# Attention and a gated MLP in one kernel: the first batch taken in one piece, two of its head groups paired

## The chip, the cores and the metric

The kernel runs on one core of one Trainium2 chip. The metric is device time in microseconds (us), the median over runs of the whole kernel. Before the change it is 391.98 us (three runs, 391.68 to 392.12).

## The reference

```python
scores = (1/sqrt(64)) * q @ k.T            # 8 batches, 12 heads, 448 tokens, 64 wide
attn   = exp(scores) / sum(exp(scores))    # the maximum is subtracted first
x      = (attn @ v) as (8*448, 768)        # tokens by all heads
h      = x @ w_in                          # 768 -> 2048
out    = (h * sigmoid(h)) @ w_out          # 2048 -> 768
```

Inputs and output are float32. The kernel loads them as float16 and gathers sums in float32.

## The kernel before

**Work.** Batches are taken one after the other. The 12 heads of a batch form three head groups of four heads (`HG = 4`, `NG = 3`). K and Q of a group are loaded with heads and 32 rows on the partitions, and VectorE turns them (`turn_k` L315, `turn_q` L333). The 448 keys form four chunks (`NCH = 4`).

**Attention of one unit.** A unit is a batch, a head group and a stretch of queries. For each key chunk, TensorE computes scores (`score`, L346) into one of two score tiles, each for two heads; ScalarE takes the exponential of each tile (`expo`, L383) into a tile `E`. A burst of scores can be *whole* (both score tiles, four heads side by side in four row strips of the array) or a *half* (one tile, two heads side by side). A half streams as many columns through the array as a whole one and does half of the work; units below `HALVES` go in halves. Then come three passes with four heads side by side in four column strips (`attend`, L409): sums (weights are ones) and two value passes (`part` 1 and 2, weights are V). VectorE turns the sums, takes the reciprocal, turns it back (L450, L458, L464) and multiplies it into the value passes (`norm`, L480), which gives the tile `xT`.

**Lone and paired head groups.** A *lone* group (`LONES`, numbered `3 * batch + group`) has its own four chunks: eight half or four whole bursts, and three passes of four chunks. In a *pair*, each group has three chunks of its own, and the fourth chunk is shared: 64 keys of each (`scores_rest`). VectorE adds the three E tiles of a group (`add_e`, L394), so the sums of both groups take three matmul steps (`attend_sums`, L425). Before the change groups 0 to 3 are lone: batch 0 and the first group of batch 1.

**Batch 0.** Its queries are cut into two pieces of 224 (`PIECES`), so it has six units of 224 queries, all lone. A burst covers two chunks (`per_burst`). Units 0 to 5 go in halves.

**The MLP.** `ffn1` multiplies `xT` by w_in in 16 blocks `f` of six matmuls each (L492, by way of `times`); ScalarE takes tanh (L518), VectorE multiplies (`gate`, L553). Batch 0 does this once for each piece, 224 columns at a time. The second product (`plain`, then `product`, also L492) goes to the output. With `strips` set, a matmul over 128 weight columns is cut into four of 32 columns, which run side by side; this avoids a change of the array's mode next to the passes of attention.

**What sets the order.** The order of all instructions is fixed when the kernel is built: `Order` keeps assumed durations and due times for TensorE, ScalarE, VectorE and the loads, and the loop at the end always issues what its clock says is ready. Each engine then runs its list strictly in that order and waits where data is late. While TensorE would have nothing to do before the first `ffn1`, the loop issues matmuls of zeros (`run_zeros`, L1468). All loads go through POOL's queue in the order of the `plan_k`, `plan_q`, `plan_v`, `plan_w_in`, `plan_w_out` calls; the queue has eight counters, so a load waits until the load eight places ahead of it has landed. V of batch 0 comes as four loads for all three groups.

```python
if qk is not None and qk <= od.now and (od.now >= pace["next"] or moe_i is None):
    run_qk()                          # a burst of scores
elif moe_i is None and av is not None and av <= od.now:
    run_av()                          # a pass of sums or values
```

Of the kernel before, what the change touches and what calls it, by code (L numbers as in the profile page):

```python
# [17 lines left out]
PE_OUT = 0.20  # L18
HOP = 0.10
DMA_ROW = 0.022  # L20
DMA_RATE = 13570.0
# [60 lines left out]
class Order:  # L82
# [19 lines left out]
    def start(self, op):  # L102
        self.emit(op.emit)
        self.free[op.eng] = self.now + op.busy
        self.busy[op.eng] += op.busy
        op.done = self.now + op.busy + op.tail
        if op.then:
            op.then(op.done)
# [61 lines left out]
def kernel(  # L170
# [29 lines left out]
    PACE = 2.6  # L200
    LONES = (0, 1, 2, 3)
    NPL = 4
    EAGER = 1
    HALVES = 6
    NEAR, LATE = 0.15, -2.0
# [4 lines left out]
    TWB, SXB = 40, 4  # L210
    PIECES = ((0, 7), (7, TPP))
    NE, NX3, NT_ = 9, 6, 2
# [129 lines left out]
    def score(pS, n, c, e, h, x0, x1, p0):  # L342
        b, hg, g0, g1 = units[n]
        nq = 32 * (g1 - g0)
        at = nq * (c % per_burst(n))
        nc.tensor.matmul(  # L346
            out=pS[p0 : p0 + 32 * (x1 - x0), h % 2, at : at + nq],
            lhsT=KT[(b, hg)][32 * h : 32 * (h + 1), c, x0:x1, :, e],
            rhs=QT[n][32 * h : 32 * (h + 1), e],
            start=(e == 0),  # L350
            stop=(e == 1),
        )


    def per_burst(n):
        return 2 if units[n][0] == 0 else 1

    def scores(n, w, ys):
        score_banks(n, w, ys)
        for c in range(per_burst(n) * w, per_burst(n) * (w + 1)):  # L360
            for e in range(2):
                for y in ys:
                    for h in (2 * y, 2 * y + 1):
                        score(pS_t[(n, w, y)], n, c, e, h, 0, rows_of(n, c) // 32, 0)


    def scores_rest(n):
        score_banks(n, 3, (0, 1))
        for e in range(2):
            for h in range(HG):  # L370
                pS = pS_t[(n, 3, h // 2)]
                score(pS, n, 3, e, h, 0, 2, 0)
                score(pS, n + 1, 3, e, h, 2, 4, 64)
# [4 lines left out]
    def expo(n, w, y):  # L378
        kr = rows_of(n, w * per_burst(n))
        nk = 32 * (units[n][3] - units[n][2]) * per_burst(n)  # L380
        if (n, w) not in E:
            E[(n, w)] = sb.tile([128, HG, S], FP16, name=f"E_{n}_{w}", tag="E", bufs=NE)
        nc.scalar.activation(  # L383
            out=E[(n, w)][0:kr, 2 * y : 2 * y + 2, 0:nk],
            in_=pS_t[(n, w, y)][0:kr, :, 0:nk],
            func=AF.Exp,
            scale=attn_scale,
        )
# [12 lines left out]
    def attend_mm(a, n, part, c, h, k0, k1, e, start, stop):  # L401
        b, hg, g0, g1 = units[n]
        nq = 32 * (g1 - g0)
        at = nq * (c % per_burst(n))
        if part == 0:
            w = ones[k0:k1, :]
        else:
            w = VT[b][k0:k1, HG * hg + h, c, part - 1 :: 2]
        nc.tensor.matmul(  # L409
            out=a[32 * h : 32 * (h + 1), 0:nq],  # L410
            lhsT=w,
            rhs=e[k0:k1, h, at : at + nq],
            start=start,
            stop=stop,
        )
# [16 lines left out]

    def attend(ns, part, n):
        if part == 0 and len(ns) == 2:
            attend_sums(ns)
            return
        acc[(n, part)] = ps.tile([128, 512], FP32, name=f"a_{n}_{part}", tag="m", bufs=4)
        for c in range(NCH):
            e = E[(ns[0] if c == NCH - 1 else n, c // per_burst(n))]
            for h in range(HG):  # L440
                attend_mm(
                    acc[(n, part)], n, part, c, h, 0, rows_of(n, c), e, c == 0, c == NCH - 1
                )
# [335 lines left out]
    for b in range(B):  # L779
        for g0, g1 in PIECES if b == 0 else ((0, TPP),):  # L780
            units += [(b, hg, g0, g1) for hg in range(NG)]
    NU = len(units)
# [38 lines left out]

    NB0 = NG * len(PIECES)
    for hg in range(NG):
        plan_k(0, hg)
        plan_q(hg)
    plan_v(0, 0, NG)
    plan_q(NG)
    plan_q(NG + 1)
    plan_w_in(0, DFF // 2)
    plan_q(NG + 2)  # L830
    plan_k(1, 0)
    plan_q(NB0)
    plan_w_in(DFF // 2, DFF)
    plan_k(1, 1)
    plan_q(NB0 + 1)
    plan_w_out(0, NFF // 4)
    plan_w_out(NFF // 4, NFF // 2)
    plan_k(1, 2)
    plan_q(NB0 + 2)
    for hg in range(NG):  # L840
        plan_v(1, hg, hg + 1)
    plan_w_out(NFF // 2, 3 * NFF // 4)
    plan_w_out(3 * NFF // 4, NFF)
    for n in range(NB0 + NG, NU):
        b, hg = units[n][:2]
        plan_k(b, hg)
        plan_q(n)
        plan_v(b, hg, hg + 1)
# [222 lines left out]
    def sums_w(ms):  # L1071

        for m in ms:
            w_op[m] = [
                od.add(
                    Op(
                        "DVE",
                        0.9,
                        lambda m=m, f0=f0: combine_w(m, f0, f0 + 4),
                        ld_wout  # L1080
                        + list(plain_op.values()) * (m == 7)
                        + [w_op[k][f0 // 4] for k in {6: (5,), 4: (6,)}.get(m, ())],
                        30,
                    )
                )
                for f0 in (0, 4)
            ]

    def queue_plain(t, j):
# [6 lines left out]
        def queue(f0, f1):  # L1096
# [17 lines left out]
            def deps():  # L1114
                if len(parts) < f0 // NPL:
                    return [None]
                made = [ld_wout[i] for i in range(len(ld_wout)) if wout_rows[i] < f1]
                for f in range(f0, f1):
                    x = g_op.get((0, f), ())
                    if len(x) < len(PIECES):  # L1120
                        return [None]
                    made += x
                return made
# [19 lines left out]
    def plan_sums():  # L1143
# [4 lines left out]
        if len(todo) == 4:  # L1148
            gates = {}
            for b in batches(qd):  # L1150
                for f in range(NFF):
                    if len(g_op.get((b, f), ())) < (len(PIECES) if b == 0 else 1):
                        return
                    gates.setdefault(f, []).extend(g_op[(b, f)])
            gates_of[qd] = gates
        gates = gates_of[qd]
        while todo and (todo[0] == 7 or sg_ring.can(1, od.now)):
# [4 lines left out]
            for f0 in (0, 4):  # L1162
                deps = [x for f in range(f0, f0 + 4) for x in gates[f] + gates[f + HF]]
                if m != 5:
# [4 lines left out]
                            "DVE",  # L1169
                            0.34,  # L1170
                            lambda m=m, f0=f0: combine_g(qd, m, f0, f0 + 4),
# [116 lines left out]
    for ns in jobs:  # L1288
        if len(ns) == 1:
            split = ((0,), (1,)) if ns[0] < HALVES else ((0, 1),)  # L1290
            qk_seq += [(ns, c, ys) for c in range(NCH // per_burst(ns[0])) for ys in split]
        else:
            split = ((0,), (1,)) if ns[0] < HALVES else ((0, 1),)
            qk_seq += [([n], c, ys) for n in ns for c in range(NCH - 1) for ys in split]
            qk_seq.append((ns, 3, (0, 1)))
        av_seq += [(ns, 0, ns[0])] + [(ns, part, n) for n in ns for part in (1, 2)]
    pace = {"next": 0.0}
# [18 lines left out]
    def run_qk():  # L1316
# [4 lines left out]
        if ys[0] == 0:  # L1321
# [3 lines left out]
            "PE",  # L1325
            2 * per_burst(n) * mm(nq) + (0.03 if rest else 0.013),
            (lambda: scores_rest(n)) if rest else (lambda: scores(n, c, ys)),
            tail=PE_OUT,
        )
        op.half = len(ys) == 1  # L1330
        if c == NCH // per_burst(n) - 1 and ys[-1] == 1:
            done = []
# [6 lines left out]
        for y in ys:  # L1339
            made = od.add(  # L1340
                Op(
                    "ACT",
                    act(2 * nq * per_burst(n)),
                    lambda y=y: expo(n, c, y),
                    [op],
                    tail=0.2,
                    then=s_ring.give,
# [25 lines left out]
    def av_at():  # L1373
        if not av_seq:
            return None
        ns, part, n = av_seq[0]
        if len(ns) == 2 and part == 0:
# [6 lines left out]
        deps = []  # L1384
        if len(exp_op.get(n, ())) < 2 * NCH // per_burst(n):
            return None
        for i, x in enumerate(exp_op[n]):
            deps.append((x, i // 2 * per_burst(n) * mm(32 * (units[n][3] - units[n][2]))))
        if part:
            deps += [(x, LATE * (units[n][0] == 0)) for x in ld_v[units[n][:2]]]  # L1390
            if units[n][0] > 0:
                deps += [(x, 0.9) for x in rdn_op.get(n, [None])]
        at, m = when(deps), m_ring.when(1)
        return None if at is None or m is None else max(at, m)

    def run_av():
        ns, part, n = av_seq.pop(0)
        b, hg, g0, g1 = units[n]
        nq = 32 * (g1 - g0)
        two = len(ns) == 2  # L1400
        m_ring.take()
        op = Op(
            "PE",
            (3 if two and part == 0 else 4) * mm(nq) + 0.013,
            lambda: attend(ns, part, n),
            tail=PE_OUT,
        )
        if part == 2:

            def then(at):  # L1410
                for _ in range((3 + (n == ns[1])) if two else NCH // per_burst(n)):
                    e_ring.give(at)
# [7 lines left out]
        if part == 0:  # L1420
            after_sums(ns, op, nq)
        else:
            after_av(n, part, op, nq)
# [135 lines left out]
```

## Time and profile before

| what | us |
|---|---|
| median of the runs shown | 391.98 |
| the profiled execution | 392.65 |
| its span (first to last instruction) | 390.8 |
| TensorE (PE) busy | 384.9 |
| VectorE (DVE) busy | 274.6 |
| ScalarE (ACT) busy | 253.8 |
| matmuls of zeros, on the chain that ended last | 2% of the span |

The profiled execution took 1.85 us more than its span, and 0.67 us more than the median. PE means matmuls, PEld weight loads, POOL the engine that issues the loads. In a row of the timeline the first number is the start, the second the time until the last of the group has ended; a group's last matmul ends some 0.2 us after the next group may start, because matmuls are pipelined. The granted TensorE clock is 1.00 in every stage.

### The profile page before, as it was taken

What the parts mean: (1) busy time and instruction counts of PE and PEld (TensorE: products, weight loads), DVE (VectorE), ACT (ScalarE), POOL (GpSimd) and SP (SyncE); (2) the same over time, 40 slices, a digit from 0 to 9 for tenths busy, and PEclk for the clock granted to TensorE, in tenths of its full rate; (3) what the DMA queues carried; (4) which work ended last, traced back from release to release, by engine and by line L of the source; (5) the groups of instructions that cost most, each with busy time, mean ns of one, the idle gap of its engine ahead of it and who ended that gap; (6) DMA issues with size and microseconds to landing.
All of it is one profiled execution on the core that took longest, in us unless ns stands there. A gap on an engine that the chain in (4) does not pass through costs nothing.

```text
span 390.8 us, 10670 instructions
## 1 busy us (share of the span) xinstructions
PE 384.9 (98%) x4369; PEld 206.8 (53%) x4369; DVE 274.6 (70%) x570; ACT 253.8 (65%) x399; POOL 89.1 (23%) x173
## 2 busy tenths in 40 slices
PE   8999999999999999999999999999999999999995
PEld 7657774444444444545445444544445655556663
DVE  2466676999996887887678758666869984447441
ACT  4987885697875779666674766566793338892120
POOL 6632456415006242400643015000000000000000
PEclk9999999999999999999999999999999999999999
DMA  7999999929039582914856129102100131001333
GB/s 116 202 210 210 162 166 180 182 43 142 3 56 148 118 109 37 129 41 93 129 92 89 47 68 164 16 0 54 32 0 3 39 92 33 0 1 38 91 96 102
DMA packets 35330, 34.52 MB, mean 88 GB/s; under 512 B 11345, under 2 KB 33745, under 8 KB 35281
## 3 DMA queue, kind: packets, MB, share of 16 engines
q0 software_dynamic: 24784, 22.82, 39.7%
q1 hardware_dynamic: 10080, 10.53, 9.9%
q8 instruction: 34, 0.56, 0.6%
q10 hardware_dynamic: 416, 0.49, 0.4%
q14 instruction: 16, 0.12, 0.1%
HBM read 45.61 MB, written 11.01 MB: 145 GB/s over the span
## 4 chain that ended last, share of the span: by engine, by line
PE 98%; ACT 1%; issue 0%; DVE 0%
PE p L492 31%; PE h L492 29%; PE s L346 13%; PE a L409 11%; PE f L492 8%; PE o L492 3%; PE z L1468 2%; PE a L425 2%; ACT E L383 1%; ACT ost L768 0%; ACT th L518 0%; DVE zeros L228 0%
## 5 line engine op out<-in xcount | busy, mean ns | idle before, releaser
L383 ACT ACTIVATE E<-s 128x896 f16<-128x896 f32 (+1 forms) x172 | 149.8, 915 | 38.5 <-PE s L346 37.0
L492 PE MATMUL h<-xT,w_in_t 128*32 128x448 f16 (+2 forms) x1086 | 117.1, 336 | 0.0
L492 PEld LDWEIGHTS <-w_in_t 128*128 128x128 f16 (+1 forms) x1158 | 71.1, 97 | 56.3 <-issue 11.5
L518 ACT ACTIVATE th<-h 128x448 f16<-128x448 f32 (+1 forms) x112 | 54.2, 493 | 36.7 <-PE h L492 31.0
L553 DVE SCALAR_TENSOR_TENSOR G<-th,h 128x448 f16<-128x448 f16 (+2 forms) x112 | 55.6, 508 | 23.4 <-ACT th L518 21.7
L492 PEld LDWEIGHTS <-G 128*128 128x128 f16 (+1 forms) x580 | 43.1, 98 | 32.4 <-issue 4.6
L768 ACT COPY ost<-p 128x384 f32<-128x384 f32 x52 | 25.0, 480 | 53.5 <-PE p L492 47.1
L346 PE MATMUL s<-rq,KT 32*128 32x448 f16 (+4 forms) x768 | 51.0, 338 | 0.5 <-ACT E L383 0.4
L280 POOL DMA_DIRECT2D V<-in_v_dram x88 | 48.3, 559 | 13.6 <-DMA w_out_t<-in_moe_w_out_dram 6.5
L492 PE MATMUL p<-w_out_t,G 128*128 128x384 f16 (+1 forms) x352 | 49.5, 326 | 0.0
L409 PE MATMUL a<-E,V 128*32 128x448 f16 (+2 forms) x864 | 42.3, 333 | 0.0
L492 PEld LDWEIGHTS <-S 128*128 128x128 f16 (+1 forms) x408 | 30.0, 98 | 22.7 <-issue 2.3
L261 POOL DMA_DIRECT2D rq<-in_q_dram x27 | 15.1, 558 | 103.9 <-PE s L346 83.1
L492 PE MATMUL p<-D,S 128*128 128x384 f16 (+1 forms) x256 | 37.1, 326 | 0.0
L480 DVE SCALAR_TENSOR_TENSOR xT<-a,rdn 128x448 f16<-128x448 f32 (+1 forms) x54 | 30.4, 568 | 6.4 <-PE a L409 4.4
L774 DVE TENSOR_TENSOR ost<-p,ost 128x384 f32<-128x384 f32 x39 | 21.6, 554 | 18.7 <-PE p L492 13.6
L346 PEld LDWEIGHTS <-KT 32*128 32x128 f16 (+2 forms) x864 | 17.5, 99 | 28.9 <-issue 27.6
L409 PEld LDWEIGHTS <-V 128*32 128x32 f16 (+1 forms) x864 | 20.5, 96 | 18.8 <-issue 7.6
L394 DVE TENSOR_TENSOR T<-E,E 128x1792 f16<-128x1792 f16 x20 | 21.7, 1083 | 8.1 <-ACT E L383 7.9
L394 DVE TENSOR_TENSOR T<-T,E 128x1792 f16<-128x1792 f16 x20 | 21.7, 1083 | 5.7 <-ACT E L383 5.7
L315 DVE STREAM_TRANSPOSE KT<-rk 128x256 f32<-128x256 f32 (+3 forms) x48 | 16.6, 384 | 7.2 <-DMA rk<-in_k_dram 6.4
L492 PE MATMUL p<-w_out_t,S 128*128 128x384 f16 (+1 forms) x152 | 19.1, 326 | 0.0
(67 smaller groups left out, 321.9 us busy)
## 6 DMA issues: line engine op xcount, KB each, us to landing
out_dram<-ost SPq DMA_DIRECT2D x194, 48.0 KB, 1.6
rk<-in_k_dram POOLq DMA_DIRECT2D x24, 224.0 KB, 5.6
rq<-in_q_dram POOLq DMA_DIRECT2D x21, 224.0 KB, 5.8
w_in_t<-in_moe_w_in_dram POOLq DMA_DIRECT2D x6, 512.0 KB, 11.1
w_out_t<-in_moe_w_out_dram POOLq DMA_DIRECT2D x4, 768.0 KB, 13.5
V<-in_v_dram POOLq DMA_DIRECT2D x43, 64.0 KB, 3.9
V<-in_v_dram POOLq DMA_DIRECT2D x40, 48.0 KB, 4.2
rq<-in_q_dram POOLq DMA_DIRECT2D x6, 112.0 KB, 6.1
```

The source lines that it names most:

```text
L280: nc.gpsimd.dma_start(out=VT[b][32 * x : 32 * (x + 1), hs, 0:count, :], in_=v[b, hs].rearrange("h (i g) d -> i h g d", g=TPP)[:, :, first ...
L315: nc.vector.transpose(out=pairs[:, x:y, 0:count], in_=t[:, first : first + count * (y - x)].rearrange("p (x c) i -> p x c i", c=count),)
L346: nc.tensor.matmul(out=pS[p0 : p0 + 32 * (x1 - x0), h % 2, at : at + nq], lhsT=KT[(b, hg)][32 * h : 32 * (h + 1), c, x0:x1, :, e], rhs=QT[ ...
L383: nc.scalar.activation(out=E[(n, w)][0:kr, 2 * y : 2 * y + 2, 0:nk], in_=pS_t[(n, w, y)][0:kr, :, 0:nk], func=AF.Exp, scale=attn_scale,)
L394: nc.vector.tensor_tensor(out=T[n], in0=T[n] if step else E[(n, 0)], in1=E[(n, step + 1)], op=ALU.add,)
L409: nc.tensor.matmul(out=a[32 * h : 32 * (h + 1), 0:nq], lhsT=w, rhs=e[k0:k1, h, at : at + nq], start=start, stop=stop,)
L480: nc.vector.scalar_tensor_tensor(out=x3(b, cc)[:, cc % 3, 32 * g0 : 32 * g1], in0=acc[(n, part)][:, 0:nq], scalar=0.5, in1=rdn_t[n].rearra ...
L492: nc.tensor.matmul(out=out[i : i + cut], lhsT=w[:, i : i + cut], rhs=x, start=start, stop=stop, skip_group_check=True,)
L518: nc.scalar.activation(out=th, in_=h_t[(b, f, t0)][:, 0 : t1 - t0], func=AF.Tanh)
L553: nc.vector.scalar_tensor_tensor(out=dst[:, f, at + lo : at + hi], in0=th_t[(b, f, t0)][:, lo - t0 : hi - t0], scalar=1.0, in1=h_t[(b, f, ...
L768: nc.scalar.copy(out=ost(qd, *OUT[m]), in_=bank(qd, BANK[m]))
L774: nc.vector.tensor_tensor(out=t, in0=bank(qd, BANK[m]), in1=t, op=ALU.add)
```

## The change

- `PIECES` and `per_burst` go. Batch 0 has three units of 448 queries, a burst covers one chunk, and each block of `ffn1` for batch 0 is 448 columns wide.
- `LONES` becomes (2, 3): groups 0 and 1 of batch 0 are a pair, group 2 is lone. `HALVES` becomes 3 (the three units of batch 0), and the shared chunk of the first pair goes in halves too.
- V of batch 0 is loaded by head group. Loads come in the order K0 Q0 K1 Q1 V0 V1 K2 Q2, half of w_in, V2, then K and Q of batch 1, the rest of w_in, and on as before.
- `attend` takes a range of chunks. The value passes of the first pair's first unit are cut: chunks 0 to 2 of both are listed ahead of the pair's sums, the shared chunk after them.
- The assumed durations of the order change: work on ACT and DVE may start 0.09 and 0.07 us before its predecessor ends (`OVERLAP`), an exponential's result counts 0.06 us after its end and no longer 0.2, and `combine_w` and `combine_g` take 0.95 and 0.40 and no longer 0.9 and 0.34.

```diff
+OVERLAP = {"ACT": 0.09, "DVE": 0.07}
...
-        self.free[op.eng] = self.now + op.busy
+        self.free[op.eng] = self.now + op.busy - OVERLAP.get(op.eng, 0.0)
...
-    LONES = (0, 1, 2, 3)
+    LONES = (2, 3)
...
-    HALVES = 6
+    HALVES = 3
...
-    PIECES = ((0, 7), (7, TPP))
...
-    def scores_rest(n):
-        score_banks(n, 3, (0, 1))
+    def scores_rest(n, ys):
+        score_banks(n, 3, ys)
         for e in range(2):
-            for h in range(HG):
+            for h in range(2 * ys[0], 2 * ys[-1] + 2):
...
-    def attend(ns, part, n):
+    def attend(ns, part, n, c0, c1):
...
-    for hg in range(NG):
+    for hg in range(2):
         plan_k(0, hg)
         plan_q(hg)
-    plan_v(0, 0, NG)
+    for hg in range(2):
+        plan_v(0, hg, hg + 1)
+    plan_k(0, 2)
+    plan_q(2)
+    plan_w_in(0, DFF // 2)
+    plan_v(0, 2, 3)
+    plan_k(1, 0)
     plan_q(NG)
-    plan_q(NG + 1)
-    plan_w_in(0, DFF // 2)
-    plan_q(NG + 2)
-    plan_k(1, 0)
-    plan_q(NB0)
     plan_w_in(DFF // 2, DFF)
...
-            qk_seq.append((ns, 3, (0, 1)))
-        av_seq += [(ns, 0, ns[0])] + [(ns, part, n) for n in ns for part in (1, 2)]
+            qk_seq += [(ns, 3, ys) for ys in split]
+        whole = [(ns, part, n, 0, NCH) for n in ns for part in (1, 2)]
+        if ns[0] == 0:
+            av_seq += [(ns, part, 0, 0, NCH - 1) for part in (1, 2)]
+            whole[:2] = [(ns, part, 0, NCH - 1, NCH) for part in (1, 2)]
+        av_seq += [(ns, 0, ns[0], 0, NCH)] + whole
...
-                    tail=0.2,
+                    tail=0.06,
```

## The prediction

> **What bounds the kernel now.** First I read the engines' busy times and the chain that ended last: TensorE is 98% of both. Next the waits of TensorE over the whole span, which are three, and none after 28.7 us. So beyond the first stage the time is what TensorE has to stream, and only the first stage is open to something else. Its timeline is next.
>
> ```profile
> PE 98%; ACT 1%; issue 0%; DVE 0%
> ```
> ```profile
> PE z L1468 <- DVE zeros L228: 1.0, 1, 1.0
> PE a L409 <- issue: 0.5, 1, 0.5
> PE s L346 <- ACT E L383: 0.4, 1, 0.4
> ```
> ```profile
> 13.27 0.57 PE L346 MATMUL s<-rq,KT 32*128 32x224 f16 x8
> 13.77 0.40 PE L1468 MATMUL z<-zeros 128*128 128x128 f16 x4
> 14.10 0.57 PE L346 MATMUL s<-rq,KT 32*128 32x224 f16 x8
> ...
> 16.27 0.57 PE L409 MATMUL a<-E,V 128*32 128x224 f16 x16
> 16.77 0.57 PE L346 MATMUL s<-rq,KT 32*128 32x224 f16 x8
> ...
> 30.31 0.75 PE L492 MATMUL h<-xT,w_in_t 128*128 128x224 f16 x6
> ```
>
> The reader is to see three prices. A half burst (8 matmuls of 224, two side by side) streams 896 columns, 0.373 us at 2400 columns per us, and the next group starts 0.50 us after it: a change of the array's mode costs some 0.12. A pass of 16 also takes 0.50. Four zeros and a change take 0.33. And the first MLP matmul (h) stands at 30.31: the border between the two stages. The chain of waits gives the dense prices:
>
> ```profile
> 203.11 3.40 PE h L492 x72
> ...
> 206.51 3.03 PE a L409 x64
> ...
> 318.75 31.21 PE f L492 x165
> ...
> 351.83 35.11 PE p L492 x216
> ```
>
> 72 column-strip matmuls of 448 are 18 steps of 0.189 us: 0.1867 of columns and 0.0026 more. The last matmul ends at 351.83 + 35.11 = 386.94.
>
> **Part one: from the first h to the end.** I count the instruction lists of both kernels, columns divided by how many matmuls run side by side. Before: 332.05 us of columns, 1994 steps, 158 changes of mode. With 0.0026 a step (5.2 us) the measured 386.94 - 30.31 = 356.63 leaves 19.4 us, 0.123 a change; the 13.77 row agrees. After: 330.56 us, 1884 steps, 155 changes. The difference is -1.49 - 0.29 - 0.37 = **-2.15 us**. It has plain sources. Before, the last piece's three passes (12 steps of 224, 1.12 us) still lie behind the first h, and so does the first burst of batch 1 (0.37); after, both lie ahead of it. The 110 steps are these 14 and the 96 that vanish as `ffn1` of batch 0 goes 448 wide. All later batches have the same columns; only their order differs.
>
> What must keep up there: ACT has 16 tanh of 0.546 in place of 32 of 0.363, 2.9 us less. Two exponentials take 1.73 and can start 0.67 after their burst (25.08 to 25.75), so a burst needs 2.4 from the one before. Batch 1's bursts stand at least 2.6 apart (two h blocks of 1.14 and a burst, or one and a pass). DVE's gates are 16 of 0.615 in place of 32 of 0.382. I cost both at nothing; TensorE's own work is the cover, 0.2 us at its thinnest. If that cover fails on all six bursts of batch 1's first pair, it is about 1 us.
>
> **Part two: up to the first h.** TensorE's list ahead of it streams 14.37 us in place of 14.56. Pairing takes one chunk in eight off, 22 half bursts for 24, and one step in four off the pair's sums. Against that come the passes and the burst of batch 1 named above, the zeros 51 + 48 for 47 + 40, and 43 changes of mode for 49. After: 1.0 (the start) + 51 x 0.109 (the first zeros, 5.13 us for 47) + 48 x 0.053 + 14.37 + 0.2 + 43 x 0.123 = 29.0 us if nothing waits. The same sum before is 29.25, and the measured 30.31 has 1.06 of waits. So I walk after's list with ACT beside it: exponentials 0.83 apart (five in 4.17, the last 0.915), the first 0.67 after its burst. ACT's timeline has that pace:
>
> ```profile
> 6.86 4.17 ACT L383 ACTIVATE E<-s 128x896 f16<-128x896 f32 x5 [4.83 <-PE s L346]
> ```
>
> - Q0 comes whole, 224 KB for 112. K0 had landed by 4.85; by bytes (368 KB moved by 5 us, 150 a us then) Q0 lands near 6.6. Its turn is 0.63 (row: 0.619), so the first burst stands at 7.3, not 6.13, and the zeros end at 6.6: 0.6 of waiting.
> - The first six exponentials pace TensorE: 7.95 to 13.0, 0.6 of waiting in spite of the zeros.
> - The seventh burst follows at 12.25, and then the first early value pass (three steps, 0.57) at 13.0, held by the sixth exponential and by V0, next paragraph.
> - From there TensorE is the slower of the two: a burst and a pass are 1.2 us, and ACT's 22nd exponential starts at 27.1, not at the 25.5 that 0.83 apart would give. Waits sum to 0.5.
> - The pair's sums need both T tiles (four adds of 1.083, two behind the sixth exponential, two behind the twelfth, ready at 19.9) and are reached at 20.1. The turn, reciprocal and turns back (0.65, 0.32, two of 0.62) hide behind the 18th burst; the lone group's chain and its last norm (0.62) end at 31.2, and the sixth matmul of h needs that at 31.6.
>
> h then starts at 29.0 + 1.7 = 30.7 us: **+0.4**. The early drawing of the two passes is in this: it fills 0.55 each where zeros would stand.
>
> **The loads.** POOL's order ahead of w_in now is K0 Q0 K1 Q1, four V0, four V1, K2, Q2, and each waits for the load eight ahead. In POOL's timeline of before, the eleventh load (a Q) shows such a wait, for the second K, the third load:
>
> ```profile
> 8.54 0.57 POOL L261 DMA_DIRECT2D rq<-in_q_dram  x1 [1.47 <-DMA rk<-in_k_dram]
> ```
>
> V0's last byte is the 1147th KB; before moved that much by 9.9, and its four first V loads landed some 1.6 us after their byte (issue to landing 7.4 and 7.9). So V0 is there at 11.5, for 13.0. K2 is issued at 11.2, when its counter is free; the first K took 3.6 from issue to landing, so 14.8, Q2 0.8 later; by the walk they delay nothing up to 16.5 and 17.3. The queue may run dry from 10.4 to 12.2, and then all later loads land about 1 us later. K and Q of batch 1 (24.9, 26.1 before) are wanted at 28.5. w_in's halves (23.7, 33.6) at 30.7 and 43. w_out's second half (issued 49.0 and 49.8, 7.5 and 10.9 to landing: 57.3, 61.5) at 59.7 and 64.3. All are covered, w_out by 1.4 us when the shift is taken off. The extra memsets (two of 0.31) and five more POOL issues (eight V more, three Q fewer, 0.55 each) lie in POOL's own time: it waits on counters there.
>
> **Sum.** -2.15 + 0.4 = -1.75: a span of 389.05 and, with the 1.85 outside it, 390.9 for the profiled execution, which was 392.65. The median shown stands 0.67 below that: 391.98 - 1.75 = **390.2**. The walk's own bounds: no waiting at all gives h at 29.0 and 388.5; each 1 us of later V0, K2 or w_out adds up to 1 us.
>
> [...] 72 more steps of h and 20 of o go in column strips, 8 of p fewer. By the rows a strip step costs 0.189, as the whole one does (165 f in 31.21 us), so this costs nothing. [...] Were four strip loads of 97 ns (row: L492 PEld 128*32, mean 97) to stand one behind the other, a step would need 0.39 us; 84 more such steps would add 17 us, 407. The 203.11 row says they do not: 72 strips in 3.40.
>
> **The rivals.**
> - *V0 or K2 late* (slower). Place: the seventh burst is followed, on TensorE's strict list, by the pass that waits for all four V0 loads; all bursts and so all exponentials queue behind it. Beyond 13.0 us each us costs one. For: small V loads had up to 11.1 to landing (one of 32 KB), and V0's last is issued near 5.5, so 16.6 and +3.6: 393.8. Likewise K2 by the 8.6 median of K loads in the first 45 us: 19.8, +3.1, 393.3. It turns the sign when V0 is later than 14.8 or K2 than 18.3. Against: in this stretch loads follow their bytes. 0.13.
> - *The first stage does not wait.* Q0 lands with K0 and the walk's 0.6 + 0.6 shrink: 388.5 to 389.5. Against: ACT's pace of 0.83 and 22 exponentials. 0.16.
> - *The gain is given back later.* A list made with other durations lets TensorE wait for ACT, DVE or w_out somewhere in 300 us, where before it waits nowhere: 1 to 2 us, 391.2 to 392.2. For: exponentials now count 0.14 sooner. Against: TensorE's changes cost 0.123 where the order assumes 0.094, so over 155 of them the other engines gain room. 0.15.
> - *The strips' weights*: 407. 0.01.
> - *Forecast*, 389.5 to 391.1: 0.55.
>
> **Chances and range.** 0.2% is 0.8 us, about what a measurement of this kernel can tell from no change. Faster by more: the forecast, the early start, and a little of the give-back: 0.72. Within: most of the give-back, 0.14. Slower: 0.14. The range holds the forecast, the early start's upper half and the give-back: 388.9 to 392.2.
>
> **What would show it.** Right: h starts near 30.7; the first burst near 7.3; the first value pass near 13.0 without a wait for V; from h to the last matmul 354.5 us with no TensorE wait; the ACT row of exponentials back to back only up to the seventh. Wrong: a TensorE wait for a V or K load before 20 us, a wait at o near 59 or 64 us, or waits for ACT between h blocks.

## The result and the profile after

The changed kernel takes 393.85 us (median of 19 executions, 391.93 to 398.41); the kernel before, beside it, takes 392.07 (19 executions, 391.65 to 392.49). The ratio is 1.0057, with a 95% interval of 1.0041 to 1.0074: slower by 0.6%, where 390.2 was forecast. The spread is the first oddity: 6.5 us, where before has 0.8. This ratio and the later ones leave out executions more than 1.5% above the fastest of their kernel, here the two at 398.37 and 398.41.

The profiled execution took 395.92, its span 394.1. Its chain that ended last, and its waits of TensorE, look nearly as before; only 2% of the span now belong to a DMA, 4.15 us of it to the landing of the very first Q:

```profile
PE 95%; DMA 2%; DVE 1%; ACT 1%; issue 1%; POOL 0%; DVEq 0%; POOLq 0%
```
```profile
PE s L344 <- DVE rq L333: 1.1, 1, 1.1
PE z L1468 <- DVE zeros L228: 1.0, 1, 1.0
PE s L344 <- ACT E L377: 0.6, 1, 0.6
```

By this view TensorE waits no longer than 0.2 us anywhere behind 9 us (the fourth row, for VectorE, in the dense part). The chain in order of time runs through TensorE alone from 8.39 us to the first MLP matmul, but for one exponential of 0.93. Still that matmul is late. The timeline of TensorE (start, duration, then line, operation, tile and count):

```profile
6.82 0.58 PE L344 MATMUL s<-rq,KT 32*128 32x448 f16 x8 [1.05 <-DVE rq L333]
...
10.82 0.57 PE L344 MATMUL s<-rq,KT 32*128 32x448 f16 x4
11.33 0.35 PE L1468 MATMUL z<-zeros 128*128 128x128 f16 x3
11.63 0.93 PE L344 MATMUL s<-rq,KT 32*128 32x448 f16 x4
12.49 0.29 PE L1468 MATMUL z<-zeros 128*128 128x128 f16 x1
12.71 1.31 PE L402 MATMUL a<-E,V 128*32 128x448 f16 x12
...
35.88 1.30 PE L488 MATMUL h<-xT,w_in_t 128*128 128x448 f16 x6
```
```profile
355.15 35.12 PE p L488 x216
```

h stands at 35.88 and not at 30.7. From there to the last matmul (355.15 + 35.12 = 390.27, by the chain) it is 354.39. The third and fifth row show the same burst, four matmuls of 448, once in 0.57 and once in 0.93 us: TensorE itself became slow. The clock row of the page (forty slices of 9.85 us) and the windows say how (columns: busy time and instructions of PE, PEld, DVE, ACT and POOL, then the granted clock, the DMA share, GB/s):

```profile
PEclk9559999999999999999999999999999999999999
```
```profile
8.00:12.00 4.00, 3.57 (x30) 1.39 (x29) 2.23 (x4) 4.00 (x6) 1.81 (x4) 0.94 0.98 128
12.00:16.00 4.00, 4.00 (x37) 0.83 (x33) 1.57 (x3) 2.39 (x4) 4.00 (x7) 0.50 0.99 143
16.00:20.00 4.00, 4.00 (x26) 1.21 (x22) 2.05 (x4) 2.64 (x4) 1.20 (x3) 0.50 0.98 139
20.00:24.00 4.00, 4.00 (x33) 1.11 (x34) 1.09 (x1) 2.82 (x4) 0.55 (x1) 0.50 1.12 208
```

The granted clock is exactly half from 12 us on; in finer windows it falls at 11.53 and returns at 28.60. In before it is 1.00 there:

```profile
8.00:12.00 4.00, 4.00 (x67) 2.55 (x64) 2.65 (x9) 3.70 (x5) 2.55 (x5) 1.00 1.33 187
12.00:16.00 4.00, 4.00 (x60) 2.75 (x62) 1.18 (x3) 4.00 (x6) 1.79 (x3) 1.00 1.31 204
16.00:20.00 4.00, 4.00 (x100) 2.53 (x96) 1.81 (x5) 3.71 (x5) 2.62 (x4) 1.00 1.12 209
```

The last column is the second thing to see: loads move 128, 143 and 139 GB/s from 8 to 20 us, where before moved 187, 204 and 209. Over the three windows that is 0.76 MB less in 12 us, some 3.6 us of loading at 209.

The mean granted clock of each execution sorts the 19: 14 lie below 0.995, five at 0.996 or more. A mean of 0.998 can still be the full clock in the first stage: a profiled execution with that mean (e10 below) shows 1.00 in every window from 4 to 36 us. The three at 0.998 or more took 391.93, 393.10 and 393.66. So a second loss is there at full clock too.

### The profile page after: what moved, and what is told of

Its sections match the earlier page's. It is cut to its first block, busy times and chain, and to the rows that moved or that the text cites. A ratio compares the mean times of both kernels' runs of the same rounds, so it can differ in the third digit from the quotient of the medians.

```text
span 394.1 us, 10432 instructions
## 1 busy us (share of the span) xinstructions
PE 387.3 (98%) x4277; PEld 191.4 (49%) x4277; DVE 272.0 (69%) x538; ACT 249.7 (63%) x381; POOL 92.0 (23%) x180
## 4 chain that ended last, share of the span: by engine, by line
PE 95%; DMA 2%; DVE 1%; ACT 1%; issue 1%; POOL 0%; DVEq 0%; POOLq 0%
PE p L488 29%; PE h L488 28%; PE s L344 13%; PE a L402 10%; PE f L488 8%; PE o L488 3%; DMA rq<-in_q_dram 2%; PE a L418 2%; PE z L1468 1%; ACT E L377 0%; DVE rq L333 0%; POOL rk L255 0%; DVE sT L446 0%; DVE ost L770 0%; ACT ost L764 0%
## 5 line engine op out<-in xcount | busy, mean ns | idle before, releaser
L377 ACT ACTIVATE E<-s 128x896 f16<-128x896 f32 (+1 forms) x170 | 146.8, 915 | 39.3 <-PE s L344 38.7
L488 PE MATMUL h<-xT,w_in_t 128*32 128x448 f16 (+1 forms) x1206 | 116.6, 353 | 0.0
L488 PEld LDWEIGHTS <-w_in_t 128*32 128x32 f16 (+1 forms) x1278 | 62.9, 97 | 62.6 <-issue 10.3
L514 ACT ACTIVATE th<-h 128x448 f16<-128x448 f32 x96 | 52.4, 545 | 36.4 <-PE h L488 32.7
L549 DVE SCALAR_TENSOR_TENSOR G<-th,h 128x448 f16<-128x448 f16 (+1 forms) x96 | 53.7, 567 | 22.3 <-ACT th L514 21.2
L280 POOL DMA_DIRECT2D V<-in_v_dram x96 | 52.3, 553 | 18.6 <-DMA w_out_t<-in_moe_w_out_dram 6.0
L344 PE MATMUL s<-rq,KT 32*128 32x448 f16 (+2 forms) x672 | 50.9, 379 | 1.8 <-DVE rq L333 1.1
L402 PE MATMUL a<-E,V 128*32 128x448 f16 (+1 forms) x768 | 43.7, 368 | 0.2 <-DVE ost L770 0.2
L476 DVE SCALAR_TENSOR_TENSOR xT<-a,rdn 128x448 f16<-128x448 f32 x48 | 28.5, 615 | 4.1 <-PE a L402 3.0
L344 PEld LDWEIGHTS <-KT 32*128 32x128 f16 (+2 forms) x768 | 12.7, 98 | 32.0 <-issue 29.9
L315 DVE STREAM_TRANSPOSE KT<-rk 128x256 f32<-128x256 f32 (+3 forms) x48 | 16.5, 383 | 7.9 <-DMA rk<-in_k_dram 7.7
```

The lines of the kernel that those rows point to most:

```text
L280: nc.gpsimd.dma_start(out=VT[b][32 * x : 32 * (x + 1), hs, 0:count, :], in_=v[b, hs].rearrange("h (i g) d -> i h g d", g=TPP)[:, :, first ...
L315: nc.vector.transpose(out=pairs[:, x:y, 0:count], in_=t[:, first : first + count * (y - x)].rearrange("p (x c) i -> p x c i", c=count),)
L344: nc.tensor.matmul(out=pS[p0 : p0 + 32 * (x1 - x0), h % 2, 0 : 32 * (g1 - g0)], lhsT=KT[(b, hg)][32 * h : 32 * (h + 1), c, x0:x1, :, e], r ...
L377: nc.scalar.activation(out=E[(n, w)][0:kr, 2 * y : 2 * y + 2, 0:nk], in_=pS_t[(n, w, y)][0:kr, :, 0:nk], func=AF.Exp, scale=attn_scale,)
L402: nc.tensor.matmul(out=a[32 * h : 32 * (h + 1), 0:nq], lhsT=w, rhs=e[k0:k1, h, 0:nq], start=start, stop=stop,)
L476: nc.vector.scalar_tensor_tensor(out=x3(b, cc)[:, cc % 3, 32 * g0 : 32 * g1], in0=acc[(n, part)][:, 0:nq], scalar=0.5, in1=rdn_t[n].rearra ...
```

## The experiments

Three theories were tried. **Clock**: gaps between the first bursts carry too few zeros, so the clock is halved. **Load**: Q of batch 1 comes too late. **List**: pairing, early passes or the refitted durations cost time by themselves. The table gives, for each kernel, its executions, how many ran at a mean clock below 0.995 and how many at 0.995 to 0.997, the median of all and of those at 0.998 or more, and how many the ratio leaves out. Where that is many (e4, e8), the ratio tells little of the kernel. The experiments e1 to e4, e5 to e8 and e9 to e12 ran on three different chips; on each, before takes 392.15 or 392.16 (median at 0.998 or more).

| kernel | executions | below 0.995 | 0.995 to 0.997 | median, us | at 0.998 or more, us | ratio to before | left out |
|---|---|---|---|---|---|---|---|
| after | 19 | 14 | 2 | 393.85 | 393.10 | 1.0057 [1.0041, 1.0074] | 2 |
| e1_more_zeros | 12 | 0 | 1 | 392.89 | 392.88 | 1.0025 [1.0010, 1.0039] | 0 |
| e2_next_kq_early | 12 | 6 | 0 | 392.42 | 390.74 | 0.9996 [0.9968, 1.0025] | 3 |
| e3_zeros_and_kq | 5 | 0 | 0 | 393.31 | 393.31 | 1.0032 [1.0020, 1.0045] | 0 |
| e4_before_few_zeros | 14 | 6 | 0 | 391.32 | 391.22 | 0.9976 [0.9966, 0.9986] | 6 |
| e5_kq_early_zeros_to_13 | 12 | 5 | 0 | 391.15 | 390.30 | 0.9984 [0.9956, 1.0012] | 1 |
| e6_no_early_passes | 4 | 2 | 2 | 395.03 | none | 1.0079 [1.0054, 1.0104] | 0 |
| e7_old_durations | 10 | 1 | 4 | 393.41 | 392.72 | 1.0023 [1.0003, 1.0044] | 1 |
| e8_lone_in_one_piece | 10 | 8 | 1 | 400.56 | 391.84 (one) | 1.0044 [1.0021, 1.0067] | 7 |
| e9_kq_early_double_to_13 | 5 | 0 | 0 | 390.76 | 390.76 | 0.9964 [0.9951, 0.9978] | 0 |
| e10_kq_early_first_zeros | 12 | 3 | 0 | 391.23 | 390.83 | 0.9978 [0.9961, 0.9996] | 1 |
| e11_kq_early_both | 10 | 0 | 0 | 390.95 | 390.95 | 0.9974 [0.9964, 0.9983] | 0 |
| e12_kq_early_double_to_20 | 11 | 0 | 0 | 391.79 | 391.79 | 0.9990 [0.9981, 0.9998] | 0 |

**e1: more zeros in after.**

```diff
-        for _ in range(n):
+        for _ in range(n if n > 40 else 2 * n + 1):
```

> The changed kernel with 2n+1 zero matmuls for every n in each gap of the first stage (99 become some 210); all else stands in the same order. Clock theory (the first stage leaves TensorE so idle between 8 and 12 us that its granted clock is halved from 11.5 to 28.6 us, which puts the first h at 35.9): the clock is 0.997 or more in every execution, the spread of 391.9 to 398.4 shrinks to under 1 us, and the median falls to some 392, where the late Q of batch 1 holds the first h near 33. Rival (loads only: the clock is a bystander): spread and median as in the changed kernel, 393.9, or worse by the zeros.

No execution lay below 0.995. The spread is 3.0 us, though, and not under 1, and the median 392.89 for some 392. The profiled execution (394.77) had h at 33.75, and now a load shows on VectorE's timeline:

```profile
30.11 0.70 DVE L315 STREAM_TRANSPOSE KT<-rk 128x384 f32<-128x384 f32 x2 [3.50 <-DMA rk<-in_k_dram]
31.21 0.65 DVE L333 STREAM_TRANSPOSE rq<-rq 128x448 f32<-128x448 f32 x1 [0.40 <-DMA rq<-in_q_dram]
31.78 0.61 DVE L446 STREAM_TRANSPOSE sT<-a 128x448 f32<-128x448 f32 x1
```

K and Q here are batch 1's. They stand ahead of the lone group's sums (sT) on VectorE's strict list, and so hold everything up to h. Keeping the clock up doesn't by itself give the forecast.

**e2: K and Q of batch 1 earlier.**

```diff
     plan_q(2)
+    plan_k(1, 0)
+    plan_q(NG)
     plan_w_in(0, DFF // 2)
     plan_v(0, 2, 3)
-    plan_k(1, 0)
-    plan_q(NG)
```

> The changed kernel with K and Q of batch 1's first group loaded ahead of the first half of w_in, not behind it and V2. Loads theory (the turn of that Q, on VectorE's strict list ahead of the lone group's sums, holds the first h; it landed at 31.4 us): the median falls by 2 us or more to some 391.5 and the fastest executions to 390.3. Clock theory alone: executions with a halved clock stay at 395 to 398, because there TensorE comes later than the Q; the median stays at 393 to 394. If both act, the fastest fall to 390.5 and the slow ones stay.

Its executions fall in two heaps, as was expected if both causes act: six at full clock, 390.08 to 391.39, and six below 0.995, 393.45 to 398.52. The profiled one, at full clock, took 390.66; sT follows its sums at once, and h stands at 31.23:

```profile
27.61 0.65 DVE L446 STREAM_TRANSPOSE sT<-a 128x448 f32<-128x448 f32 x1 [2.88 <-PE a L402]
```
```profile
349.88 35.11 PE p L488 x216
```

The last matmul ends at 384.99; the span is 388.9. Two bursts of batch 1 stand ahead of h here and one in after (0.50 us each), so 31.23 here corresponds to the forecast's 30.7. At full clock the late loads cost 393.10 - 390.74 = 2.4 us, by medians of three and six executions; after's three lie 1.7 us apart.

**e3: both.**

> Both edits together. Clock theory and loads theory together: no halved clock, first h at 31.5 to 32.5 (some 2 us of zeros more than in the forecast, which had 30.7), 391.0 to 392.0 with a spread under 1 us. If only the loads mattered: 391.5 with a spread; if only the clock: as with the zeros alone, 392.

All at full clock, within 0.7 us of each other, and behind the first burst no load is waited for; but at 393.31 this misses the expected time by over 1 us, and h stands at 34.86, for 31.5 to 32.5. Doubled everywhere, zeros make TensorE the late one: sT starts at 31.05 and has waited 3.88 us for TensorE, where in e2 it starts at 27.61. Zeros are free here only where something else sets the pace: these cost 2.6 us (393.31, where e2 has 390.74 at full clock).

**e4: the kernel before, with one zero for each call of `run_zeros` after the first.**

```diff
-        for _ in range(n):
+        for _ in range(n if n > 40 else 1):
```

> The kernel before the change with one zero matmul in each gap of the first stage after the first 47 (40 become 12). Clock theory: the granted clock falls below 1 in some executions and the time spreads to 394 and above, as with the change. Rival (the zeros do nothing, the change's loads are the cause): 392.0 as before with a spread of 0.8, or 0.5 less.

A gap can hold several calls: by the trace 23 zeros are left of 40, and not the 12 that were expected. This kernel separates the clock from everything else in the change. Eight executions at full clock took 391.10 to 391.35, six took 402.55 to 405.52. A window of the profiled one, which took 404.18 and was at half clock from 11.94 to 42.66 us:

```profile
15.00:18.40 3.40, 3.40 (x33) 2.00 (x33) 0.81 (x2) 2.38 (x4) 0.00 (x0) 0.50 1.11 208
```

So the zeros taken out cost some 0.9 us (392.16 for before beside it, 391.22 here) and hold the clock. Not quite always: beside these experiments before itself took 406 to 410 in 7 of 85 executions, at mean clocks of 0.948 to 0.956.

**e5: e2, and two zeros more in each gap between 6 and 13 us.**

```diff
+            n += 2 * (6.0 < od.now < 13.0)
             od.on_pe(Op("PE", n * each, lambda n=n: run_zeros(n)), "full")
```

> The kernel after with two edits: K and Q of batch 1's first group are loaded ahead of w_in, as in the run before this one that did that alone (390.1 to 391.4 at full clock, 393.5 to 398.5 where the clock was halved), and each gap that the order fills with zeros between its 6 and 13 us gets two zeros more; gaps later than that get none more. Clock theory: what is missing is TensorE's activity from 8 to 12 us only; the dozen more zeros (0.053 us each, some 0.7 us) lie in gaps where the exponentials pace TensorE. So every execution at a clock of 0.995 or more, and 390.3 to 391.3, faster than before by 0.2 to 0.4%. Rival one, zeros cost what they stream: full clock but 391.5 or more, as with the edit that doubled all the zeros (393.3). Rival two, the halving starts from a stretch behind 13 us: executions at 393.5 and over remain.

Five of twelve stayed below 0.995: a miss. The edit lets the order plan with the zeros, and the order then moved things: the gaps hold 8, 0, 13, 3 and 6 zeros, where after has 6, 2, 3, 2 and 3. In the profiled execution Q0 was late as well; TensorE waited 2.1 us ahead of its first burst, and the clock was half from 8.72 to 18.96 us. Two explanations were open: thin gaps, or the idle time ahead of a late first burst.

**e6, e7, e8: one part of the change undone at a time**, in after: the early passes, the durations (0.2, 0.9 and 0.34 go back as well), the pairing.

```diff
-        if ns[0] == 0:
-            av_seq += [(ns, part, 0, 0, NCH - 1) for part in (1, 2)]
-            whole[:2] = [(ns, part, 0, NCH - 1, NCH) for part in (1, 2)]
...
-OVERLAP = {"ACT": 0.09, "DVE": 0.07}
+OVERLAP = {}
...
-    LONES = (2, 3)
+    LONES = (0, 1, 2, 3)
```

> The kernel after without the two value passes drawn ahead of the shared chunk: both run whole behind the pair's sums. Clock theory: from 12.7 to 16 us two passes of 0.57 us give way to gaps with two or three zeros, TensorE streams less there, so the halving comes at least as often as in after (about half of the executions), and the passes are paid for behind 20 us: median 393.5 to 396. Rival, the strict list waits for V: bursts are freed of the wait for V's loads and the exponentials run on at their pace, median 392.5 or less. By the trace of after no load was waited for at these passes, so I expect the first.

395.03, in the expected range, but the profiled execution shows a cause that the expectation didn't have. Its passes now follow the burst of batch 1, which waits for Q:

```profile
31.02 0.80 PE L344 MATMUL s<-rq,KT 32*128 32x448 f16 x8 [2.92 <-DVE rq L333]
31.75 3.09 PE L402 MATMUL a<-E,V 128*32 128x448 f16 x32
```
```profile
28.00:32.00 4.00, 1.08 (x14) 0.26 (x16) 2.32 (x6) 0.15 (x1) 3.14 (x5) 0.90 1.13 209
32.00:36.00 4.00, 4.00 (x41) 1.61 (x33) 1.70 (x3) 1.58 (x2) 1.05 (x2) 0.67 1.09 195
```

2.92 us without work, and right behind it the clock is half from 31.21 to 34.62 us (0.90, then 0.67 as means of four us). So this late load was paid twice. The one stretch of 3.41 us gives this execution a mean of 0.995. At 0.995 to 0.997 lie 10 of the 55 executions of kernels whose loads for batch 1 come late (after, e1, e6, e7, e8), and none of 67 with these loads early. That fits a halving behind the late load there too, but no trace other than e6's shows one. The early passes take work out of the stretch behind the late load; that they gain isn't shown, as e6 has four executions, all below 0.998, and its interval overlaps that of after.

> The kernel after with the order's durations as before the change (no overlap on ACT and DVE, 0.2 after an exponential, 0.9 and 0.34 for the combines). My theory: the list up to 14 us and the loads stay, so do the halving and the late Q of batch 1, and the dense stage waits nowhere in after: 393 to 395, within 0.3% of after. Rival, the refitted durations make a worse list: 392.5 or less.

The time came as expected, the halving did not: one of ten below 0.995, where after has 14 of 19. Four more lie at 0.995 and 0.996 (393.53 to 395.04). And the one, which is the profiled execution, had TensorE wait 2.03 us ahead of its first burst and was at half clock from 8.58 to 35.89 us, so the clock fell ahead of the gaps between the bursts. In the list that the old durations give, these gaps hold 8, 3, 4, 3 and 3 zeros. The refit made the order believe that exponentials follow each other sooner, so it put 6, 2, 3, 2 and 3 there. At full clock e7 takes 392.72 and after 393.10, medians of five and three: the rest of the refit moves nothing that these runs can tell.

> The kernel after with groups 0 to 3 lone as before the change, batch 0 still in one piece, loads as in after. TensorE streams two half bursts and one more step of sums, about 1.2 us with their changes of mode. Theory: the bursts up to 12.7 us are the same, so the halving stays as frequent; at full clock the late Q of batch 1 hides a part of the extra 1.2 us: 392.5 to 394.5 at full clock, 395 to 399 where halved. Rival, the pair's long row of bursts without passes is what leaves TensorE idle: full clock in all executions and 392 to 393.5.

Eight of ten below 0.995, most at 399 to 402, more than expected: in the profiled execution the clock is half from 10.06 to 37.36 us. Why so much longer than in after, no run shows. Pairing isn't what lowers the clock.

**e9 to e12: which zeros it takes.** All have e2's loads; the zeros are added without the order counting them, so its list stays e2's. The three lines are those of e9, e10 and e11; e12 is e9 with 20 for 13.

```diff
+            nz = 2 * n + 1 if n < 40 and od.now < 13 else n
+            nz = n + 10 * (n > 40)
+            nz = n + 10 if n > 40 else 2 * n + 1 if od.now < 13 else n
-            od.on_pe(Op("PE", n * each, lambda n=n: run_zeros(n)), "full")
+            od.on_pe(Op("PE", n * each, lambda n=nz: run_zeros(n)), "full")
```

> K and Q of batch 1 early, and each gap of zeros up to the order's 13 us gets 2n + 1 zeros for n; later gaps as in after. In the run before this one, two more zeros a gap left 5 of 12 executions below a clock of 0.995, and the profiled one had its first burst at 8.2 us, held 2.1 us by Q. Theory one, the thin zeros from 8 to 13 us lower the clock and two more a gap were too few: no execution below 0.995, 390.3 to 391.5. Theory two, TensorE's idle time ahead of a late first burst lowers it: some 4 of 12 executions stay below 0.995, at 394 and over. The nine zeros in place of four ahead of the first burst fill 0.3 us of that idle time, so theory two allows somewhat fewer.

> K and Q of batch 1 early, and ten more zeros (0.53 us) only ahead of the first burst. Theory two (idle time ahead of the first burst): no or one execution of twelve below 0.995, the rest 390.2 to 391.3. Theory one (thin zeros from 8 to 13 us): about half below 0.995, 393.5 to 398.5, as without the ten.

> K and Q of batch 1 early, ten more zeros ahead of the first burst and 2n + 1 for n in the gaps up to 13 us. If both stretches count, only this one and the next have no execution below 0.995. Time then 390.5 to 391.6, faster than before by 0.1 to 0.4%. If zeros cost what they stream even where exponentials pace TensorE, 392 or more.

> K and Q of batch 1 early, 2n + 1 zeros for n in the gaps up to the order's 20 us, none more after. The version with the zeros doubled in every gap had the full clock in all executions and 393.3, with the lone group's chain held by TensorE. If the zeros behind 20 us cost that (some 25 zeros, 1.3 us, and what queues behind them): 391 to 392 at full clock. If the zeros from 13 to 20 us cost it: 392.5 to 393.3. If the halving needs the zeros behind 20 us to stay away: executions below 0.99.

The gaps up to 13 us decide: e9, e11 and e12, which all have more than twice as many zeros there, have none of 26 executions below 0.995. e9's profiled execution kept its clock although TensorE waited 1.4 us for Q0, longer than in after. e10, with thin gaps and a full start, still has three of twelve; e2 without its ten zeros has six. So filling the start isn't enough; how much it helps isn't settled (three against six of twelve). That a long wait there can do harm, the traces suggest: in e5 and e7 TensorE waited 2.10 and 2.03 us ahead of the first burst, and the clock fell within 0.6 us of that burst, at 8.72 and 8.58; behind 1.86 (e6), 1.62 (e12) and 1.43 us (e9) it didn't fall. The timeline of e9 shows how dense is dense enough:

```profile
9.64 0.57 PE L344 MATMUL s<-rq,KT 32*128 32x448 f16 x4
10.14 0.62 PE L1468 MATMUL z<-zeros 128*128 128x128 f16 x8
10.69 0.56 PE L344 MATMUL s<-rq,KT 32*128 32x448 f16 x4
11.19 0.51 PE L1468 MATMUL z<-zeros 128*128 128x128 f16 x6
11.63 0.57 PE L344 MATMUL s<-rq,KT 32*128 32x448 f16 x4
```

A burst stands some 1.0 us behind the one before it, with 0.32 to 0.43 us of zeros between (6 to 8 of 0.053). In after it is 0.81, with two or three zeros (0.11 to 0.16). By columns TensorE streams 0.373 + 0.37 of each 1.0 us in e9, 0.373 + 0.13 of each 0.81 in after: 74% against 62%. (The 0.373 is 896 columns at the forecast's 2400 a us, which before's rows give: 165 steps of 448 columns in 31.21 us and 216 of 384 in 35.11 differ by 0.0266 us a step for 64 columns, 2405 a us.) The bursts fill half of the array's rows (two tiles of 32*128 side by side), the zeros all of them (128*128); taken so, it is 56% against 39%. These shares are worked out from the lists and rows; where the limit lies between them no run shows. The zeros delay e9's first value pass (13.45, after 12.71), and yet its time is e2's at full clock: e2 waits 0.46 us for V2 ahead of the lone group's value passes, at 29.09, and e9 reaches them at 29.40 without a wait. From 13 to 20 us the zeros do cost, 391.79 in e12 for 390.76 in e9, and behind 20 us more, 393.31 in e3.

**A version that beats both kernels.** e9 takes 0.36% less than before (0.22 to 0.49, five executions) and e11 0.26% (0.17 to 0.36); both leave after behind by some 3 us, and neither had an execution with a mean clock below 0.998.

## Why the prediction was wrong

- *From the first h to the end*: right. Counting columns, steps and changes of mode gave 356.63 - 2.15 = 354.48; the trace has 354.39. In this execution no wait for ACT, VectorE or w_out took it back, nor did the strips' weights cost anything. It doesn't settle the rival of the give-back, as everything behind h came 5 us later than forecast. Where h comes earlier, the cover of 1.4 us that the forecast saw at w_out can be gone: TensorE waited 1.16 us for w_out in e1's profiled execution, and in e11's, the slowest of its ten, as follows. In e2, e3, e9, e10 and e12 it didn't.

```profile
60.82 1.46 PE L488 MATMUL o<-w_out_t,G 128*128 128x384 f16 x8 [1.40 <-DMA w_out_t<-in_moe_w_out_dram]
```

- *The first bursts*: right within 0.5 us. First burst at 6.82 for 7.3, first value pass at 12.71 for 13.0, without a wait for V. The rival of a late V0 or K2 didn't come either: K2 and Q2 landed at 15.61 and 17.05, 0.8 and some 1.5 us later than forecast, and the bursts that need them stood behind others. e2 shows 0.5 us of waiting for V2, which the forecast had not priced.
- *The first h at 30.7*: failed, by 5.2 us in the profiled execution, and by two terms. They overlap: at full clock, with the loads still late, e1 has h at 33.75.
- *The first term is the clock, which the forecast took at 1.00 in every stage.* The walk counted zeros only as filler and priced each at 0.053; it wrote that the early passes stand "where zeros would stand". It never asked what fewer zeros do. Nor did the totals tell it: after has more zeros in all (51 + 48 for 47 + 40). Between the first bursts, though, after has 6, 2, 3, 2, 3 and 1 zeros and only then a pass, before 8, 2, 4 and 2 and then a pass of sums:

```profile
6.76 0.62 PE L1468 MATMUL z<-zeros 128*128 128x128 f16 x8
...
8.36 0.28 PE L1468 MATMUL z<-zeros 128*128 128x128 f16 x2
...
9.17 0.40 PE L1468 MATMUL z<-zeros 128*128 128x128 f16 x4
...
10.00 0.28 PE L1468 MATMUL z<-zeros 128*128 128x128 f16 x2
```

- e4 shows that zeros hold the clock of before, e1 and e9 that they hold it in after, with late and with early loads. In the profiled execution the chain holds no late load and one exponential behind 9 us; the delay of h is the half clock's.
- In after the clock was half from 11.53 to 28.60, 17.07 us; the other halved stretches of profiled executions lasted 3.41 to 30.72 us (last section). It took no long idle time: TensorE's longest after the start was 1.05 us there, ahead of the first burst, and from 9 us on no wait was over 0.2. What decides which executions are hit, no run shows.
- *The second term is the loads.* "All later loads land about 1 us later" was mis-sized: Q of batch 1 was turned at 31.45, for 26 to 27 forecast. The forecast's own limit for them was 28.5. With the loads early, h stands where it should (e2); what any later landing up to 28.5 would do, no run tests. What failed is the step from POOL's order to time. Two rows of POOL's timeline in after show it:

```profile
17.59 0.56 POOL L255 DMA_DIRECT2D rk<-in_k_dram  x1 [0.95 <-DMA rq<-in_q_dram]
21.90 0.55 POOL L261 DMA_DIRECT2D rq<-in_q_dram  x1 [3.75 <-DMA w_in_t<-in_moe_w_in_dram]
```

- Before issued these two at 14.02 and 16.64. Eight counters and four small V loads ahead of them made K wait for Q2, and Q for the first of the three loads of w_in's half, eight places ahead. The forecast applied that rule to V0 and K2, and not to the load with the least room behind them. Meanwhile the DMA engines ran short: from 8 to 20 us after moved 1.64 MB, before 2.40, and slices of 0.3 us fell to 12 and 17 GB/s.
- *The parts.* Early passes: forecast as a gain, which e6 (395.03 for 393.85) fits but doesn't show. Pairing: at full clock only one execution of e8 stands against it, so its worth there isn't shown. Refit: costed at nothing in the first stage; it is what thinned the zeros, and without it one of ten executions is below 0.995 (e7).
- *The forecast without the two terms* was good, in part by luck: at full clock with the early loads the medians are 390.74 (e2), 390.30 (e5) and 390.76 (e9), for 390.2. In e2 the first zeros took 4.68 us for the forecast's 5.56, and TensorE's waits ahead of h sum to 2.2 us for 1.7, with V2 among them; the two misses offset in part. The sum 390.2 + 2.4 (loads) leaves 0.5 of after's 393.10 at full clock open, about the scatter of three executions; the halved clock adds 0.75 to the median and up to 5.3 to the slowest. Two figures of the forecast are off by 0.2 us, and nothing hangs on them: the sum for before is 29.04 by its own terms and not 29.25, and a K2 at 19.8 is 3.3 us behind 16.5 and not 3.1.

## What to carry to other kernels

Where zeros keep TensorE's clock up, as e1, e4 and e9 show here, count them on both sides of a change, gap by gap, in the stretch ahead of the dense part: a list that expects other engines to be quicker puts fewer zeros there (here 6, 2, 3, 2 and 3 where the old durations gave 8, 3, 4, 3 and 3), and in after the clock halved although TensorE never waited longer than 1.05 us behind its start. A wide spread between executions with a lower mean clock was the sign of it (6.5 us in after, 14 of 19 below 0.995, where before beside it has 0.8 us); one profiled execution at full clock doesn't rule it out (e2's is at 1.00, with six of twelve below 0.995). With a queue of few counters (eight here), follow each load that has little room to the load that many places ahead of it, and take small loads for full places.

## What the runs showed of the hardware

- The half clock came with TensorE busy in the records for nearly all of the time: 3.57 of 4 us in the window where it fell, 4.00 of 4 in the windows in which it stayed half. e6 kept the full clock with TensorE busy for 3.41 of the 4 us from 8 to 12. So in these runs busy time by the profile doesn't tell when the clock falls.
- The halved stretches ahead of 60 us lasted 3.41 (e6), 10.24 (e5), 17.07 (after), 27.31 (e7), 27.30 (e8) and 30.72 us (e4); the longer ones are close to 3, 5, 8, 8 and 9 times e6's. In after the clock stayed half with TensorE busy throughout: 4.00 of 4 us in every window from 12 to 28 us. What ended these stretches, no run shows.
- In before's windows from 12 to 36 us the loads moved 204 to 211 GB/s; in after, with small V loads among them (698 packets under 512 B of 1817 from 8 to 20 us) and POOL waiting for counters, it was 137 from 8 to 20 us. Before moved 200 from 8 to 20 us, with 546 such packets of 2757. Which of the two causes counts, no run shows.
